# First MLP product by seven products of halves, attention by single head pairs in chunks of 96 tokens, raw weights in shared buffers

## The chip, the cores and the metric

One core of one Trainium2 chip. The time is the device time of the kernel in microseconds (us), the median of several executions. Executions of one kernel differ by 1 to 7 us, and the runs were made on more than one chip, so a kernel is compared by its ratio to the executions of the kernel before that were made with it. Engines: PE is TensorE's matmul stream, PEld its weight loads, DVE is VectorE, ACT is ScalarE, POOL is GpSimd, SP issues the DMAs. Everything is float32.

## The reference, cut to what matters

```python
batch, n_heads, seq, head_dim = (8, 8, 576, 64)
scores = q @ k.T / sqrt(64)
ret = scores * where(rel >= 0, gamma[h] ** rel, 0)   # rel = i - j, per head
x = (ret @ v)          # to 4608 tokens x 512
h = x @ w_in           # 512 x 2048; w_in, w_out, alpha arrive as float64
g = maximum(h, 0) + alpha * minimum(h, 0)
out = g @ w_out        # 2048 x 512
```

## The kernel before: the parts that matter here

The tokens go through the MLP in 18 blocks of 256, each in 8 units of 2 x 128 hidden columns: 144 units. Attention runs head pair by head pair (32 pairs in all), and units of blocks that are ready are put between its steps. The weights are float64 in DRAM; the kernel rebuilds float32 from the two 32-bit halves, piece by piece (32 pieces), while the first head pairs run.

```python
def load_piece(src, dst):                       # one of 32 pieces
    raw = wraw.tile([P, 2, HM, 2], INT32, tag="raw", bufs=4)
    nc.sync.dma_start(raw, src)
    lo, hi = raw[:, :, :, 0], raw[:, :, :, 1]
    a = wraw.tile([P, 2, HM], FP32, tag="wa", bufs=3)
    nc.scalar.activation(a, hi.bitcast(FP32), ACTF.Abs)
    nc.scalar.activation(lo, lo.bitcast(UINT32), ACTF.Copy, scale=2.0 ** -29)
    nc.vector.tensor_scalar(a, a, HI_MIN, HI_MAX, ALU.max, ALU.min)
    c = ps_a.tile([P, 2, HM], INT32, tag="psa")                     # in PSUM
    nc.vector.tensor_scalar(c, a.bitcast(INT32), 3, 0x3FFFFFF8, ...)
    nc.vector.scalar_tensor_tensor(out=dst, in0=hi, ..., in1=c, ...)
    nc.gpsimd.tensor_tensor(out=dst, in0=dst, in1=lo, op=ALU.add)

def mlp_unit(kb, i):
    ph = ps_h.tile([P, 2, TB], FP32, tag="psh")
    for x in range(2):
        for cc in range(NCC):                   # 8 matmuls of 256 columns
            nc.tensor.matmul(ph[:, x, :], w_in[i // UST][:, cc, x, f0:f0 + P],
                             xb[kb][:, cc, :], start=(cc == 0), stop=(cc == NCC - 1))
    # ... g: 2 scalings, 1 combination, 4 additions on VectorE
    # ... the second product of the unit before: 7 matmuls of 256 columns

for n, (b, u) in enumerate(couples):            # two head pairs at a time,
    qT, kT, rT = transposes(...)                # 4 chunks of 128 tokens + 64
    load_weights(2); pop_units(share // 3)
    at = scores(...)
    load_weights(3); states(...); pop_units(share // 3)
    values(...)
    load_weights(3); pop_units(share - 2 * (share // 3))
```

Of the kernel before, what the change touches and what calls it, by code (L numbers as in the profile page):

```python
# [18 lines left out]
def kernel(  # L19
# [10 lines left out]
    nc = tc.nc  # L30
# [6 lines left out]
    NC2 = NPAIR // 2  # L37
    C = P
    NJ = S // C
    REM = S - NJ * C  # L40
# [8 lines left out]
    UST = NU // NST  # L49

    assert D == 64 and 2 * D == P and DM == H * D and NTOK == B * S
    assert NTOK % TB == 0 and 2 * REM == P and NJ == 4
    assert NPAIR == NCC and DM == 512 and NU % NST == 0 and NC2 == 2

    const = ctx.enter_context(tc.tile_pool(name="const", bufs=1))
    wpool = ctx.enter_context(tc.tile_pool(name="wpool", bufs=1))
    wraw = ctx.enter_context(tc.tile_pool(name="wraw", bufs=2))
    xpool = ctx.enter_context(tc.tile_pool(name="xpool", bufs=6))
    nat = ctx.enter_context(tc.tile_pool(name="nat", bufs=2))
    attn = ctx.enter_context(tc.tile_pool(name="attn", bufs=1))  # L60
    mlp = ctx.enter_context(tc.tile_pool(name="mlp", bufs=2))
    ps_a = ctx.enter_context(tc.tile_pool(name="ps_a", bufs=3, space=bass.MemoryType.PSUM))
    ps_h = ctx.enter_context(tc.tile_pool(name="ps_h", bufs=1, space=bass.MemoryType.PSUM))
    ps_o = ctx.enter_context(tc.tile_pool(name="ps_o", bufs=1, space=bass.MemoryType.PSUM))

    couples = [(b, u) for b in range(B) for u in range(NC2)]



    def load_couple(b, u):  # L70
        got = []
        for name, src in (("k", k), ("q", q), ("v", v)):
            t = nat.tile([P, NJ, 4, D], FP32, tag=f"nat_{name}", name=f"{name}n_{b}_{u}")
            r = nat.tile([P, 2, D], FP32, tag=f"rem_{name}", name=f"{name}r_{b}_{u}")
            for j in range(NJ):
                nc.sync.dma_start(
                    t[:, j, :, :],
                    src[b, 4 * u:4 * u + 4, j * C:(j + 1) * C, :].rearrange("h p d -> p h d"))
            for i in range(2):
                h = 4 * u + 2 * i  # L80
                nc.sync.dma_start(
                    r[i * REM:(i + 1) * REM, :, :],
                    src[b, h:h + 2, NJ * C:S, :].rearrange("h p d -> p h d"))
            got += [t, r]
        return got

    loaded = {0: load_couple(*couples[0])}
# [13 lines left out]
    dif = const.tile([P, NBIT + 1, H], FP32, name="dif")  # L101
# [5 lines left out]
    for i in range(NBIT):  # L107
        nc.vector.scalar_tensor_tensor(out=dif[:, i + 1], in0=dif[:, i], scalar=2.0,
                                       in1=dif[:, i], op0=ALU.add, op1=ALU.mult)

    facl = const.tile([P, 2, H], FP32, name="facl")
    for o, y, i in [(fac[:, j], fac[:, j - 1], NBIT) for j in range(1, NJ)] + \
            [(facl[:, i], fac[:, NJ - 1], NBIT - i) for i in range(2)]:
        nc.vector.scalar_tensor_tensor(out=o, in0=dif[:, i], scalar=1.0, in1=y,
                                       op0=ALU.add, op1=ALU.mult)
# [5 lines left out]
    nc.vector.tensor_tensor(out=pf, in0=dif[:, 0:NBIT],  # L121
                            in1=pbit[:, :, None].to_broadcast([P, NBIT, H]), op=ALU.mult)
# [4 lines left out]


    tab = [const.tile([P, NC2, NJ, 4], FP32, name=f"tab{x}") for x in range(2)]
    tabr = const.tile([P, 2, NC2, 2], FP32, name="tabr")  # L130
    for u in range(NC2):
        hs = slice(4 * u, 4 * u + 4)
        nc.vector.tensor_tensor(out=tab[0][:, u], in0=fac[:, :, hs],
                                in1=pf[:, 0:1, hs].to_broadcast([P, NJ, 4]), op=ALU.mult)
    for i in range(2):
        rows = slice(i * REM, (i + 1) * REM)
        x, y = [t_.rearrange("p (u i h) -> p u i h", u=NC2, i=2)[:, :, i, :]
                for t_ in (facl[rows, i], pw[rows])]
        nc.vector.tensor_tensor(out=tabr[rows, 0], in0=x, in1=y, op=ALU.mult)
    for o, x in ((tabr[:, 1], tabr[:, 0]), (tab[1], tab[0])):  # L140
        nc.vector.tensor_scalar(o, x, float(np.sqrt(D)), None, ALU.mult)
        nc.vector.reciprocal(o, o)

    mask = const.tile([P, C], FP32, name="mask")
# [3 lines left out]
    maskr = const.tile([P, C], FP32, name="maskr")  # L148
    nc.gpsimd.tensor_copy(maskr, mask)
    nc.gpsimd.memset(maskr[0:REM, REM:C], 0.0)  # L150
# [3 lines left out]
    sm = const.tile([P, NJ, 2, P], FP32, name="sums")  # L154
# [9 lines left out]

    FS = UST * P
    w_in = [wpool.tile([P, NCC, 2, FS], FP32, tag=f"wi{i}", name=f"w_in{i}")
            for i in range(NST)]

# [11 lines left out]

    def load_piece(src, dst):
# [3 lines left out]
        raw = wraw.tile([P, 2, HM, 2], INT32, tag="raw", bufs=4, name=f"raw_{at}")  # L185
        nc.sync.dma_start(raw, src)
        lo, hi = raw[:, :, :, 0], raw[:, :, :, 1]
        a = wraw.tile([P, 2, HM], FP32, tag="wa", bufs=3, name=f"wa_{at}")
# [7 lines left out]
        c = ps_a.tile([P, 2, HM], INT32, tag="psa", name=f"wc_{at}")  # L196
        nc.vector.tensor_scalar(c, a.bitcast(INT32), 3, 0x3FFFFFF8,
                                ALU.logical_shift_left, ALU.bitwise_and)
        nc.vector.scalar_tensor_tensor(  # L199
            out=dst.rearrange("p x f -> p (x f)").bitcast(INT32),  # L200
            in0=raw.rearrange("p x f two -> p (x f) two")[:, :, 1], scalar=-0x40000000,
            in1=c.rearrange("p x f -> p (x f)"), op0=ALU.bitwise_and, op1=ALU.bitwise_or)
# [3 lines left out]
    def combine(i):  # L206
        w = w_out[i]
        for eng, o, x, y in ((nc.vector, 4, 1, 0), (nc.vector, 5, 3, 4),
                             (nc.gpsimd, 6, 5, 2), (nc.gpsimd, 1, 3, 1)):
            eng.tensor_tensor(out=w[:, o], in0=w[:, x], in1=w[:, y], op=ALU.subtract)  # L210

    pieces = []
    for s in range(NST):
        for cc in range(NCC):
            pieces.append((win32[cc, :, :, s * FS:(s + 1) * FS, :], w_in[s][:, cc], None))
        for i in range(UST * s, UST * (s + 1)):
            pieces.append((wout32[i], w_out[i][:, 0:2], None))
            pieces.append((wout32[NU + i], w_out[i][:, 2:4], i))

    def load_weights(n):  # L220
        for _ in range(min(n, len(pieces))):
            src, dst, unit = pieces.pop(0)
            load_piece(src, dst)
            if unit is not None:
                combine(unit)
# [5 lines left out]
    xb = {}  # L231
# [3 lines left out]
    def out_block(kb, po):  # L235
        p1, p2, p6, p7, p5, p3, p4 = [po[n // 2][:, n % 2, :] for n in range(7)]

        osb = wraw.tile([P, 2, 2, HM], FP32, tag="raw", bufs=4, name=f"osb_{kb}")
        s12 = wraw.tile([P, 2, HM], FP32, tag="wa", bufs=3, name=f"s12_{kb}")
        u3 = wraw.tile([P, HM], FP32, tag="wa", bufs=3, name=f"u3_{kb}")  # L240
# [7 lines left out]
        nc.vector.tensor_tensor(out=osb[:, 1, 0], in0=u3, in1=p4, op=ALU.subtract)  # L248
# [16 lines left out]

    def mlp_unit(kb, i):
        ph = ps_h.tile([P, 2, TB], FP32, tag="psh", name=f"ph_{kb}_{i}")
        f0 = (i % UST) * P
        for x in range(2):
            for cc in range(NCC):  # L270
                nc.tensor.matmul(ph[:, x, :], w_in[i // UST][:, cc, x, f0:f0 + P],  # L271
                                 xb[kb][:, cc, :], start=(cc == 0), stop=(cc == NCC - 1))


        g = mlp.tile([P, 8, P], FP32, tag="g", bufs=2, name=f"g_{kb}_{i}")
        neg = mlp.tile([P, 2, TB], FP32, tag="neg", bufs=1, name=f"neg_{kb}_{i}")
        for x in range(2):
            fc = x * NU + i
            nc.vector.tensor_scalar(neg[:, x], ph[:, x], 0.0, alpha[:, fc:fc + 1],  # L279
                                    ALU.min, ALU.mult)  # L280
        nc.vector.scalar_tensor_tensor(  # L281
            out=g[:, 0:4, :].rearrange("p x t -> p (x t)"),
            in0=ph.rearrange("p x t -> p (x t)"), scalar=0.0,
            in1=neg.rearrange("p x t -> p (x t)"), op0=ALU.max, op1=ALU.add)
        for o, x, y, op in ((4, 1, 3, ALU.add), (6, 0, 1, ALU.subtract),
                            (5, 4, 0, ALU.subtract), (7, 2, 5, ALU.subtract)):
            nc.vector.tensor_tensor(out=g[:, o, :], in0=g[:, x, :], in1=g[:, y, :], op=op)  # L287
        pend.append((kb, i, g))
        if len(pend) > 1:
            mlp_out()  # L290

    queue = []

# [4 lines left out]
    def put_x(c, tok, n, src):  # L298

        at = 0  # L300
        while at < n:
            kb, o = divmod(tok + at, TB)
            if kb not in xb:
                xb[kb] = xpool.tile([P, NCC, TB], FP32, tag="xb", name=f"xb_{kb}")
# [6 lines left out]
    def transposes(n, b, u, tiles):  # L311
        kn, kr, qn, qr, vn, vr = tiles
        for x, t, r in ((0, qn, qr), (1, vn, vr)):
            nc.gpsimd.tensor_tensor(
                out=r, in0=r, in1=tabr[:, x, u, :, None].to_broadcast([P, 2, D]), op=ALU.mult)
            nc.gpsimd.tensor_tensor(  # L316
                out=t, in0=t, in1=tab[x][:, u, :, :, None].to_broadcast([P, NJ, 4, D]),
                op=ALU.mult)
        qT = [attn.tile([P, NJ * C], FP32, tag=f"qT{i}", bufs=2, name=f"qT{i}_{n}")
              for i in range(2)]  # L320
        kT = [attn.tile([P, NJ * C], FP32, tag=f"kT{i}", name=f"kT{i}_{n}") for i in range(2)]
        rT = attn.tile([P, 2, C], FP32, tag="rT", bufs=2, name=f"rT_{n}")
        for src, dst in ((kn, kT), (qn, qT)):
            for i in range(2):
# [142 lines left out]
```

## Time and profile before

| | before |
|---|---|
| median time | 1200.31 us (1198.62 to 1202.2, 4 runs) |
| span of the profiled run | 1196.8 us |
| TensorE busy | 1135.9 us, 95% |
| VectorE / ScalarE / GpSimd busy | 49% / 9% / 11% |
| first 160 us: PE / DVE / POOL busy | 104.9 / 114.6 / 86.1 us |

A fp32 matmul appears as two instructions on TensorE (the 8 of the first product as 16 on its line, a row that the prediction shows). Its lines of busy shares and slices, and the stretches, are shown in the prediction. A second reading, called the split and used all through this document, was made after the result: how much time TensorE *loses in the head*. From 200 us on TensorE is full, so the time from there to its last instruction can be split: each instruction of the MLP at its own pace (0.216 us for 256 columns, 0.112 for 128), and the rest divided by the head pairs that are left (69 TensorE instructions per pair before, 90 after). Before: 992.0 us = 132.7 first products x 3.456 + 134 second products x 3.024 + 22.75 pairs x 5.63. Then the loss in the head is the span, less 4.8 us after TensorE's last start, less all 144 units, less all 32 pairs: 1196.8 - 4.8 - 144 x 6.48 - 32 x 5.63 = 78.6 us (from unrounded rates; good to some 2 us, and each from one profiled execution, so that two kernels which differ by less than some 3 us are not told apart). It is what the kernel would save if it ran from its first instant as it runs later. Unlike "when does the first unit of this number start", it doesn't depend on the order of the work.

### The profile page before, as it was taken

To read this page: it belongs to the slowest core of one execution; us is meant where nothing else is said; L and a number is where in the kernel's file an instruction comes from. 1 tells how busy PE (TensorE), PEld (TensorE's weight loads), DVE (VectorE), ACT (ScalarE), POOL (GpSimd) and SP (SyncE) were. 2 spreads that over 40 slices of the span, in tenths; PEclk is the share of its full clock that TensorE was granted. 3 is DMA by queue.
4 is the path that set the end of the run, shared out by engine and by line. 5 is a ranking of instruction groups with operands and counts; after the bars stand their busy time and mean duration, and the time that the engine had idled before them with its cause. 6 is when DMAs were issued, how large, how long until landed. Compare 5 with 4: busy or idle time off the path is not lost.

```text
span 1196.8 us, 15945 instructions
## 1 busy us (share of the span) xinstructions
PE 1135.9 (95%) x6529; PEld 984.5 (82%) x6529; DVE 584.5 (49%) x1516; ACT 110.8 (9%) x283; POOL 131.0 (11%) x125
## 2 busy tenths in 40 slices
PE   1678899999999999999999999999999999999998
PEld 1566778888888888888888888888888888888887
DVE  2788955354445363544443635363535444434444
ACT  1444300000000000001001000000000000000000
POOL 3565430000000000000000000000000000000000
PEclk8669899999999999999999999999999999999999
DMA  7777611010111010101110202020110000000000
GB/s 175 199 192 180 174 23 36 20 40 19 38 23 51 14 51 20 40 19 38 23 37 20 57 21 58 21 58 20 47 31 18 1 18 1 18 1 18 1 19 18
DMA packets 127145, 55.56 MB, mean 46 GB/s; under 512 B 116305, under 2 KB 116321, under 8 KB 127073
## 3 DMA queue, kind: packets, MB, share of 16 engines
q1 hardware_dynamic: 127072, 54.56, 17.6%
q8 instruction: 51, 0.84, 0.3%
q14 instruction: 22, 0.17, 0.0%
HBM read 45.10 MB, written 9.44 MB: 46 GB/s over the span
## 4 chain that ended last, share of the span: by engine, by line
PE 88%; DVE 3%; DMA 1%; issue 0%; POOL 0%; SPq 0%; DVEq 0%; POOLq 0%
PE ph L271 42%; PE po L259 35%; PE ps L345 2%; PE pv L388 2%; PE pv L397 2%; PE pt L327 2%; PE pu L368 1%; DVE at L349 1%; PE psr L356 1%; DMA vn<-in_v_dram 1%; PE pvr L402 0%; DVE w_out L210 0%; DVE wa L193 0%; PE pvr L392 0%; DMA qr<-in_q_dram 0%
## 5 line engine op out<-in xcount | busy, mean ns | idle before, releaser
L271 PE MATMUL ph<-xb,w_in 128*128 128x256 f32 x2304 | 534.4, 384 | 3.4 <-DVE g L281 3.4
L271 PEld LDWEIGHTS ph<-xb,w_in 128*128 128x128 f32 x2304 | 435.7, 191 | 66.2 <-DVE g L281 4.7
L259 PE MATMUL po<-w_out,g 128*128 128x256 f32 x2016 | 460.6, 380 | 2.2 <-DVE g L287 2.2
L259 PEld LDWEIGHTS po<-w_out,g 128*128 128x128 f32 x2016 | 382.7, 190 | 54.6 <-DVE g L287 2.4
L279 DVE TENSOR_SCALAR neg<-ph,alpha 128x256 f32<-128x256 f32 x288 | 126.4, 478 | 511.1 <-PE ph L271 510.9
L287 DVE TENSOR_TENSOR g<-g 128x128 f32<-128x128 f32 x576 | 162.7, 323 | 8.6
L281 DVE SCALAR_TENSOR_TENSOR g<-ph,neg 128x512 f32<-128x512 f32 x144 | 99.5, 691 | 4.8
L316 POOL TENSOR_TENSOR vn<-vn,tab 128x1024 f32<-128x1024 f32 x16 | 30.9, 1928 | 412.2 <-DMA vn<-in_v_dram 326.8
L345 PE MATMUL ps<-qT,kT 64*128 64x128 f32 x512 | 55.9, 304 | 18.5 <-DVE w_in L199 14.4
L345 PEld LDWEIGHTS ps<-qT,kT 64*128 64x128 f32 x512 | 48.1, 203 | 28.5 <-DVE w_in L199 15.4
L316 POOL TENSOR_TENSOR qn<-qn,tab 128x1024 f32<-128x1024 f32 x16 | 31.0, 1936 | 286.7 <-PE po L259 144.1
L306 ACT COPY xb<-pv 128x256 f32<-128x256 f32 (+3 forms) x88 | 21.7, 322 | 377.6 <-PE pv L397 377.5
L349 DVE TENSOR_TENSOR at<-ps,mask 128x512 f32<-128x512 f32 x64 | 41.2, 684 | 23.3 <-PE ps L345 23.3
L330 ACT COPY kT<-pt 128x512 f32<-128x512 f32 x32 | 17.6, 590 | 294.4 <-PE pt L327 294.2
L242 ACT COPY s<-po 128x256 f32<-128x256 f32 x18 | 6.7, 373 | 336.1 <-PE po L259 336.1
L388 PE MATMUL pv<-at,vn 128*64 128x128 f32 x512 | 33.6, 285 | 1.6 <-DVE w_out L199 1.6
L388 PEld LDWEIGHTS pv<-at,vn 128*64 128x64 f32 x512 | 29.5, 144 | 6.1 <-issue 4.0
L193 DVE TENSOR_SCALAR wa<-wa 128x512 f32<-128x512 f32 x32 | 20.6, 645 | 18.5 <-ACT wa L189 18.5
L377 DVE TENSOR_TENSOR sums<-pu,sums 64x128 f32<-64x128 f32 x96 | 27.7, 289 | 2.8
L397 PE MATMUL pv<-qT,sums 128*128 128x128 f32 x192 | 27.3, 287 | 0.4 <-DVE sums L377 0.2
L189 ACT ACTIVATE wa<-raw 128x512 f32<-128x512 f32 x32 | 21.5, 672 | 55.5 <-DMA raw<-in_moe_w_out_dram 35.5
L397 PEld LDWEIGHTS pv<-qT,sums 128*128 128x128 f32 x192 | 23.1, 191 | 4.2 <-issue 2.7
(70 smaller groups left out, 427.1 us busy)
## 6 DMA issues: line engine op xcount, KB each, us to landing
out_dram<-osb SPq DMA_DIRECT2D x36, 256.0 KB, 2.2
kn<-in_k_dram SPq DMA_DIRECT2D x64, 128.0 KB, 2.9
qn<-in_q_dram SPq DMA_DIRECT2D x64, 128.0 KB, 2.8
vn<-in_v_dram SPq DMA_DIRECT2D x64, 128.0 KB, 2.9
raw<-in_moe_w_in_dram SPq DMA_DIRECT2D x16, 512.0 KB, 6.1
raw<-in_moe_w_out_dram SPq DMA_DIRECT2D x16, 512.0 KB, 3.8
kr<-in_k_dram SPq DMA_DIRECT2D x32, 32.0 KB, 2.3
qr<-in_q_dram SPq DMA_DIRECT2D x32, 32.0 KB, 2.4
```

What stands on the lines that cost most here:

```text
L259: nc.tensor.matmul(acc[kb][n // 2][:, n % 2, :], g[:, x, :], w_out[i][:, y, :], start=(i == 0 and n % 2 == 0), stop=(i == NU - 1 and (n % ...
L271: nc.tensor.matmul(ph[:, x, :], w_in[i // UST][:, cc, x, f0:f0 + P], xb[kb][:, cc, :], start=(cc == 0), stop=(cc == NCC - 1))
L279: nc.vector.tensor_scalar(neg[:, x], ph[:, x], 0.0, alpha[:, fc:fc + 1], ALU.min, ALU.mult)
L281: nc.vector.scalar_tensor_tensor(out=g[:, 0:4, :].rearrange("p x t -> p (x t)"), in0=ph.rearrange("p x t -> p (x t)"), scalar=0.0, in1=neg ...
L287: nc.vector.tensor_tensor(out=g[:, o, :], in0=g[:, x, :], in1=g[:, y, :], op=op)
L316: nc.gpsimd.tensor_tensor(out=t, in0=t, in1=tab[x][:, u, :, :, None].to_broadcast([P, NJ, 4, D]), op=ALU.mult)
L327: nc.tensor.transpose(pt[:, j * C:(j + 1) * C], src[:, j, 2 * i:2 * i + 2, :].rearrange("p h d -> p (h d)"), ident)
L345: nc.tensor.matmul(ps[h2][:, cols], kT[i][rows, cols], qT[i][rows, cols], start=True, stop=True)
L349: nc.vector.tensor_tensor(out=a, in0=ps[h2].rearrange("p (j w) -> p j w", w=C), in1=mask[:, None, :].to_broadcast([P, NJ, C]), op=ALU.mult)
L377: nc.vector.tensor_tensor(out=sm[hd, j, :, hd], in0=ps[hd, j, :, :], in1=sm[hd, j - 1, :, hd], op=ALU.add)
L388: nc.tensor.matmul(pv[i][h2 * D:(h2 + 1) * D, j * C:(j + 1) * C], vn[:, j, 2 * i + h2, :], at[2 * i + h2][:, j, :], start=(j == 0), stop=F ...
L397: nc.tensor.matmul(pv[i][:, j * C:(j + 1) * C], sm[:, j - 1, i, :], qT[i][:, j * C:(j + 1) * C], start=False, stop=(j == NJ - 1), skip_gro ...
```

## The change

The second product was already a Strassen product: seven products of quarters in place of eight. The change does the same to the first one, whose products then are 128 columns wide, and needs combinations of w_in and of x for it (on GpSimd). These take memory, so attention goes to single pairs in six chunks of 96 (two score groups of three chunks), with two PSUM buffers in place of three; the raw weights lose their own buffers and use those of the output and of later x blocks.

```diff
-    def mlp_unit: 8 matmuls, 256 columns each
+        for n, (m, o, l, r) in enumerate((
+                (0, 2, 0, x[:, 0:2, 0:P]), (0, 0, 2, x[:, 2:4, 0:P]), (0, 1, 5, t[:, 1]),
+                (1, 0, 4, t[:, 0]), (1, 1, 6, x[:, 0:2, P:TB]),
+                (1, 2, 1, x[:, 2:4, P:TB]), (1, 3, 3, t[:, 2]))):
+            for cc in range(2):                 # 14 matmuls of 128 columns
+                nc.tensor.matmul(ph[m][:, o], w_in[i // UST][:, l, cc, f0:f0 + P], r[:, cc], ...)
+        # g: 1 copy on ScalarE, 4 additions out of PSUM, 2 scalings, 1 combination, 4 additions
+    S_WORK = ((6, 0, 1, ALU.subtract), (4, 1, 3, ALU.add), (5, 4, 0, ALU.subtract),
+              (1, 2, 5, ALU.subtract))          # per quarter of w_in, on GpSimd
+    def combine_x(kb): 4 subtractions of 256 elements on GpSimd per token block
     # combinations of w_out: two of four on VectorE before, all on GpSimd after
-        raw = wraw.tile(..., tag="raw", bufs=4)
-        c = ps_a.tile([P, 2, HM], INT32, tag="psa")
+        raw = ring.tile(..., tag=raw_tag(at))   # 5 shared buffers for 16 pieces, then 3
+        c = ps_h.tile([P, 2, HM], INT32, tag="psh1")   # shared with half of the first product
-    C = P                                       # chunks of 128, couples of head pairs
+    C = 96                                      # 6 chunks, single pairs
-    ps_a: bufs=3, ps_h: 1 tile
+    ps_a: bufs=2, ps_h: psh0, psh1
```
(cut to its core)

## The prediction

> **What bounds the kernel now.** I read the page's busy shares and 40 slices first. TensorE is busy 95% of the span; from slice 6 on it is full, at the full granted clock. VectorE is at half.
>
> ```profile
> PE 1135.9 (95%) x6529; PEld 984.5 (82%) x6529; DVE 584.5 (49%) x1516; ACT 110.8 (9%) x283; POOL 131.0 (11%) x125
> ...
> PE   1678899999999999999999999999999999999998
> ...
> DVE  2788955354445363544443635363535444434444
> ...
> POOL 3565430000000000000000000000000000000000
> PEclk8669899999999999999999999999999999999999
> ```
>
> So there are two stages: a head of some 160 us in which weights are unpacked and TensorE has gaps at a low clock, and a steady stage in which every nanosecond of TensorE's stream is on the path. The table of stretches shows the border:
>
> ```profile
> 60.00:90.00 30.00, 21.63 (x154) 18.32 (x155) 25.17 (x46) 13.84 (x27) 19.01 (x16) 0.67 0.72 193
> 90.00:120.00 30.00, 25.44 (x191) 20.22 (x189) 26.23 (x50) 12.90 (x27) 15.97 (x15) 0.96 0.71 180
> 120.00:150.00 30.00, 26.92 (x186) 21.30 (x186) 27.49 (x57) 11.64 (x25) 14.72 (x14) 0.89 0.68 170
> ...
> 300.00:600.00 300.00, 299.55 (x1733) 260.92 (x1732) 134.51 (x361) 17.18 (x54) 18.31 (x16) 1.00 0.12 31
> ```
>
> Its columns are busy time of matmul, weight load, VectorE, ScalarE and GpSimd, then clock, DMA share and GB/s. From 300 to 600 us TensorE idles 0.45 us. Then I read the timeline inside the steady stage, for the weight loads (PEld), whose starts are recorded:
>
> ```profile
> 704.85 3.43 PEld L271 LDWEIGHTS ph<-xb,w_in 128*128 128x128 f32 x16
> ...
> 708.30 3.00 PEld L259 LDWEIGHTS po<-w_out,g 128*128 128x128 f32 x14
> ...
> 711.32 3.43 PEld L271 LDWEIGHTS ph<-xb,w_in 128*128 128x128 f32 x16
> ```
>
> One MLP unit lasts 711.32 - 704.85 = 6.47 us: 30 instructions (each fp32 matmul is two) of 0.216 us. 16 belong to the first product, 3.45 us. The question of the whole change is what such an instruction costs with 128 moving columns in place of 256, when each still needs its own 128x128 weights. The kernel before has that case, in the attention's products with the running sums:
>
> ```profile
> 753.36 1.42 PEld L397 LDWEIGHTS pv<-qT,sums 128*128 128x128 f32 x12 [0.17 <-issue]
> ...
> 754.70 0.53 PEld L402 LDWEIGHTS pvr<-rT,sums 128*128 128x128 f32 x4
> ```
>
> L397 moves 128 columns, L402 64. One load lasts 0.19 us, so the starts are (1.42 - 0.19) / 11 = 0.112 us apart in the first and (0.53 - 0.19) / 3 = 0.113 in the second. Half the columns do not make it shorter[...].
>
> [...] these three additions, 1.02 us for four elsewhere, take 2.39 us beside a GpSimd multiply.
>
> ```profile
> 725.63 2.39 DVE L287 TENSOR_TENSOR g<-g 128x128 f32<-128x128 f32 x3
> 725.94 1.94 POOL L316 TENSOR_TENSOR qn<-qn,tab 128x1024 f32<-128x1024 f32 x1 [28.30 <-PE po L259]
> ```
>
> **The change, part by part.**
>
> First product. Removed per unit: 16 instructions of 0.216 us = 3.45 us. Added: 7 products x 2 halves x 2 = 28 of 0.112 us = 3.14 us. The gain is 0.32 us, not the eighth of 3.45 (0.43) that counting multiplications suggests[...]. Over the 138 of 144 units outside the head: 44 us less on the path. A unit becomes 6.16 us.
>
> Attention. In the chain of work in order of time, the starts of first products are 6.475 us apart except where attention lies between; over one couple of head pairs the excess is 4.05 (values), 2.10 (transposes) and 5.13 (scores and states), together 11.28 us, or 5.64 per pair. After, per pair, at the starts in the trace:
> - 12 transposes instead of 9, 0.109 us each[...]: 1.3, and 0.2 for waits on two buffers;
> - 12 score products of 96 columns. The two heads lie in separate halves of the array and run as pairs; a pair of instructions takes 0.111 us at 128 columns, so I estimate 0.084 at 96. 12 x 0.084 = 1.0, plus about 0.3 (three starts delayed by 0.1 each) on entering and leaving such a group, now two groups: 1.6;
> - 10 state products at 0.058 per pair of instructions: 0.6 + 0.3 = 0.9;
> - 12 value products of 96 columns at 0.084: 1.0; 5 with the sums, two instructions each at 0.112: 1.1; entry and exit 0.3: 2.4.
> The sum is 6.4, and 6.6 with the first wait of the states for a bank. 0.96 us more per pair, over 24 pairs after the head: +23 us on the path. Half the gain goes back here.
>
> VectorE. Per unit now: four additions out of PSUM (three of 256 elements at 0.41 as on L247, one of 128 at 0.28), two scalings of 256 in SBUF (about 0.3, an estimate from L193, whose fastest 512-element runs take 0.43), one 512-element combination (0.69) and four additions of 128 (0.26 to 0.32): 4.1 us, against 2.9 before. With the output block (7 x 0.41 per 8 units) and attention (4 x 0.45 + 5 x 0.22 per 4.5 units) that is 5.1 of some 7.6 us of TensorE time: 67%, no bound. Latency: g must be ready when the second product starts, one whole unit later, about 8 us after its first sums are complete; 4.1 us fit, also with one GpSimd multiply (1.5 us) in the way.
>
> GpSimd. Per token block four subtractions of 256 elements, about 0.65 each by a line through L314 (128 in 0.43) and L316 (1024 in 1.93): 2.6 us, and twice as many, three-quarter-size multiplies. In the compiled order the subtractions for the next block stand half a block ahead, and at a batch's border one whole unit (6 us) lies between the last copies and the first product that needs them. I allow 5 us in all for such stalls.
>
> The head. Before, it ends at 162 us with 6 units done. What paces it is a loop and not one engine: the DMA queue waits for raw buffers, as its waits up to 170 us say.
>
> ```profile
> SPq L186 <- POOL w_in L203: 41.1, 13, 7.3
> SPq L186 <- POOL qr L314: 11.1, 3, 4.6
> SPq L186 <- POOL w_out L203: 7.8, 7, 2.7
> ```
>
> After: only two single pairs are loaded ahead of the first weights, which therefore start at about 11 us instead of 22.7; five raw buffers for 16 pieces, then three instead of four; and the unpacking no longer takes the attention's PSUM buffers (before, the first scores wait 11 us for VectorE to release one). Against that, GpSimd gets the combinations of both weights: 8 x 2 x 1.5 multiplies, 32 x 1.31 additions, 32 x 0.75 and 16 x 1.07 combinations, 5 for blocks = 112 us, against 86 by 160 us before. It would be 80% busy and may set the pace. The unpacking also shares one PSUM buffer with half of the first product, so in the compiled order VectorE takes pieces and units strictly in turn. DMA bytes are the same. Earlier start minus these: the head ends at 150 us with 6 units done, plus or minus 10.
>
> Sum: 150 + 138 x 6.16 + 24 x 6.6 + 5 stalls + 5 for the last block = 1168 us of span. The same sum for before is 162 + 138 x 6.475 + 12 x 11.28 + 5 = 1196, against 1196.8 seen. The median time is about 3 us over the span: 1170 us, 2.5% less.
>
> **The rivals.**
>
> (a) The halves stream at their share of columns, 0.107 us: units of 6.02, 1151 us. Against it: L397's starts at 0.112, and L402's.
>
> (b) VectorE's longer chain[...] makes the second product wait. A stall of 0.3 us per unit would cost 41 us: 1211. For it: the collision above. Against it: 4 us of slack, and GpSimd busy only some 12% of the steady stage.
>
> (c) The head grows: GpSimd or the three raw buffers pace it, and it ends at 170 us or later: 1190, within 2%. For it: GpSimd's 112 us and the waits of the DMA queue. Against it: the start 11 us sooner.
>
> (d) With two PSUM buffers for attention instead of three, TensorE waits in each of five groups per pair: 0.3 us each would be 36 us over 24 pairs: 1206. Against it: the compiled order puts a whole unit, or three first-product matmuls, between most of these groups.
>
> **Range and chances.** Steady-stage rates are measured, so unit and attention together are good to 10 us; the head to 10; stalls can only add. I give 1150 to 1190. The border of 2% lies at 1176.8, close above my value: faster 0.63, within 2% 0.33, slower 0.04.
>
> **What would show each step.** Weight loads of the first product 0.112 us apart and units of 6.16 us between attention groups (0.107: rival a). Attention adds 6.4 to 6.6 us per pair. TensorE's idle time after 170 us under 12 us in all; if it is tens of us, with VectorE's g as releaser it is (b), with score or value copies as releaser (d). First raw weights issued at about 11 us, TensorE full from about 150; if GpSimd is full in the head and the fill comes after 165, (c). What would make it wrong most: a head much longer or shorter than 150, since its loop is the one part that I did not add up from rows.

The two heads' score products run as pairs by their starts in the trace of before, where the second follows the first by 7 ns and the next pair comes 105 to 112 later. The 0.107 us of rival (a) stand for half of the 0.216 of 256 columns; half is 0.108, and the units would be 6.05.

## The result, and the profile after

1183.81 us median (1182.47 to 1188.55, 4 runs) against 1200.31: the ratio is 0.9869, 95% interval 0.9837 to 0.9901. Ratios here are the mean time of one kernel's fast runs over that of the other's of the same rounds, so not quite the ratio of the medians quoted. That is 1.3% less: within 2%. The time lies in the predicted range, 14 us above the predicted value, and the class that was held likeliest did not come.

The page of the changed kernel, the same rows that the prediction shows of the one before:

```profile
PE 1138.2 (96%) x8929; PEld 1030.3 (87%) x8929; DVE 774.5 (66%) x2142; ACT 189.1 (16%) x547; POOL 236.4 (20%) x227
...
PE   6877899999999999999999999999999999999998
...
DVE  6558768566657576756665767676667566667565
...
POOL 4786571110111011200110201021112000100000
PEclk9998889999999999999999999999999999999999
```

TensorE is busy just as long, with 2400 instructions more; VectorE is at 66%, as worked out. The slices fill at about the same place as before: the head did not become visibly shorter. Its timeline near the end, weight loads of the first product, in rows of eight:

```profile
1155.10 1.08 PEld L285 LDWEIGHTS ph<-xb,w_in 128*128 128x128 f32 x8
1156.10 0.97 PEld L285 LDWEIGHTS ph<-xt,w_in 128*128 128x128 f32 x8
...
1161.25 1.08 PEld L285 LDWEIGHTS ph<-xb,w_in 128*128 128x128 f32 x8
```

One load takes 0.19, so in the second row the starts are (0.97 - 0.19) / 7 = 0.111 us apart, and units start 1161.25 - 1155.10 = 6.15 us apart. Stretches, with the columns of the prediction's:

```profile
20.00:40.00 20.00, 17.01 (x114) 14.73 (x113) 11.48 (x24) 10.09 (x27) 15.05 (x13) 1.00 0.67 188
40.00:60.00 20.00, 17.59 (x126) 15.39 (x127) 12.69 (x28) 10.20 (x23) 15.44 (x16) 1.00 0.69 166
...
300.00:600.00 300.00, 299.40 (x2411) 272.24 (x2411) 196.69 (x554) 39.54 (x126) 39.45 (x36) 1.00 0.13 34
```

In the steady stage TensorE is idle for 0.6 of 300 us, so VectorE does not hold it up. (Busy time is modelled, 0.28 us for an instruction of the first product where the starts are 0.112 apart, and so hides short waits; by the starts of the instructions, the two PSUM buffers cost some 0.3 us per pair, as shown below.) Split as before, the changed kernel has 976.6 us from 200 us = 133.1 x 3.136 + 135 x 3.024 + 23.38 pairs x 6.45. The sums of both spans, side by side:

| part | before | predicted | after |
|---|---|---|---|
| 144 units | 144 x 6.48 = 933.1 | 144 x 6.16 = 887.0 | 144 x 6.16 = 887.0 |
| 32 head pairs | 32 x 5.63 = 180.3 | 32 x 6.6 = 211.2 | 32 x 6.45 = 206.5 |
| lost in the head | 78.6 | 60.2 (150 - 6 x 6.16 - 8 x 6.6) | 83.0 |
| stalls, last block | 4.8 | 5 + 5 | 4.9 |
| span | 1196.8 | 1168.4 | 1181.4 |

Units came as predicted; pairs and stalls cost 10 us less. The whole miss, and more, is in the head: it was to lose 18 us less than before, and lost 4 more. Its DMA queue's waits up to 200 us answer to those shown of before:

```profile
SPq L179 <- POOL w_out L194: 46.4, 10, 10.7
SPq L179 <- POOL w_in L194: 43.9, 13, 9.6
SPq L76 <- PE pu L377: 24.1, 6, 7.7
SPq L76 <- PE pv L391: 18.8, 7, 12.1
```

The weights did start sooner (first raw piece issued at 8.1 us, landed at 13.0; before 22.7 and 27.4), but the last one landed at 160.7 us (before 145.2). At this place DMA waits for the unpacking and not the unpacking for DMA: piece 12 (counted from 0) landed at 57.3 us, and ScalarE took it up at 73.8. The start that was gained is used up half way. GpSimd's addition to the 4th, the 16th and the last piece starts at 44.5, 86.3 and 152.1 us before, and at 28.2, 85.6 and 171.2 us in the changed kernel.

One thing stands in no row of the page. Ten instructions with the running sums, in the chain of waits, once in the head and once in the steady stage (start, us, what):

```profile
33.70 2.39 PE pv L395 x10
...
514.85 1.28 PE pv L395 x10
```

In the head TensorE runs at half rate: these instructions, with full 128 x 128 weights, start 213 ns apart instead of 112. By the durations of the weight loads (0.34 us in place of 0.19) this lasts from 8 to 81 us almost without a break, and some 90 us in all; in the kernel before some 60 us (58 by its granted clock, 0.82 over the first 160, and 3 before that record begins). The row of the granted clock reads 1.00 through those 80 us. It is not blind to the state: the first change of the clock that this trace records is the one to full rate at 81.3 us, and before it the row shows 1.00. In a run told of below, which has recorded changes from 6.5 us on, the same stretch has the same work at 0.50:

```profile
20.00:40.00 20.00, 17.01 (x115) 14.50 (x114) 11.81 (x23) 10.90 (x27) 15.58 (x14) 0.50 0.65 192
```

So where no change is recorded yet, go by the durations. What brings TensorE from half rate to full is not shown, nor which property of the attention work keeps it there: it was busy 17.0 and 17.6 of 20 us in the two stretches above, with small gaps, and stayed at half rate.

### The profile page after: what moved, and what is told of

Read it like the earlier page. It is cut to its first block, busy times and chain, and to the rows that moved or that the text cites. A ratio compares the mean times of both kernels' runs of the same rounds, so it can differ in the third digit from the quotient of the medians.

```text
span 1181.4 us, 22020 instructions
## 1 busy us (share of the span) xinstructions
PE 1138.2 (96%) x8929; PEld 1030.3 (87%) x8929; DVE 774.5 (66%) x2142; ACT 189.1 (16%) x547; POOL 236.4 (20%) x227
## 4 chain that ended last, share of the span: by engine, by line
PE 85%; DVE 7%; POOL 3%; issue 2%; ACT 1%; DMA 1%; SPq 0%; DVEq 0%; POOLq 0%; ACTq 0%
PE ph L285 37%; PE po L255 34%; PE ps L366 4%; PE pv L395 3%; PE pv L391 3%; PE pt L354 3%; PE pu L377 2%; DVE wa L186 1%; POOL xt L270 1%; DVE g L307 1%; DVE wc L190 1%; POOL vn L345 1%; DVE g L296 1%; POOL xb L270 1%; DVE w_out L192 1%
## 5 line engine op out<-in xcount | busy, mean ns | idle before, releaser
L296 DVE TENSOR_TENSOR g<-ph,g 128x256 f32<-128x256 f32 (+1 forms) x576 | 211.7, 388 | 314.5 <-ACT g L291 168.8
L285 PE MATMUL ph<-xb,w_in 128*128 128x128 f32 x2304 | 333.5, 283 | 4.2 <-DVE g L296 3.3
L285 PEld LDWEIGHTS ph<-xb,w_in 128*128 128x128 f32 x2304 | 294.5, 194 | 14.0 <-POOL w_in L194 2.9
L285 PE MATMUL ph<-xt,w_in 128*128 128x128 f32 x1728 | 248.3, 279 | 7.0 <-POOL xt L270 2.8
L285 PEld LDWEIGHTS ph<-xt,w_in 128*128 128x128 f32 x1728 | 221.4, 195 | 8.9 <-POOL xt L270 3.1
L299 DVE TENSOR_SCALAR g<-g,alpha 128x256 f32<-128x256 f32 x288 | 120.3, 459 | 4.9
L301 DVE SCALAR_TENSOR_TENSOR g<-g 128x512 f32<-128x512 f32 x144 | 105.8, 735 | 4.2
L366 PEld LDWEIGHTS ps<-qT,kT 64*96 64x96 f32 x768 | 52.1, 179 | 24.3 <-issue 12.8
L366 PE MATMUL ps<-qT,kT 64*96 64x96 f32 x768 | 64.3, 278 | 3.9 <-DVE at L369 3.2
L369 DVE TENSOR_TENSOR at<-ps,mask 96x288 f32<-96x288 f32 x128 | 53.2, 446 | 10.3 <-PE ps L366 10.2
```

What stands on the lines that cost most here:

```text
L285: nc.tensor.matmul(ph[m][:, o], w_in[i // UST][:, l, cc, f0:f0 + P], r[:, cc], start=(n in (0, 3) and cc == 0), stop=(n in (2, 6) and cc = ...
L296: nc.vector.tensor_tensor(out=o, in0=x0, in1=x1, op=ALU.add)
L299: nc.vector.tensor_scalar(g[:, 4 + 2 * m:6 + 2 * m], g[:, 2 * m:2 * m + 2], 0.0, alpha[:, fc:fc + 1], ALU.min, ALU.mult)
L301: nc.vector.scalar_tensor_tensor(out=g[:, 0:4].rearrange("p x t -> p (x t)"), in0=g[:, 0:4].rearrange("p x t -> p (x t)"), scalar=0.0, in1 ...
L366: nc.tensor.matmul(ps[h2][:, j], kT[rows, c0:c0 + C], qT[rows, c0:c0 + C], start=True, stop=True)
L369: nc.vector.tensor_tensor(out=at[h2][:, r * JR:(r + 1) * JR], in0=ps[h2], in1=mask[:, None, :].to_broadcast([C, JR, C]), op=ALU.mult)
```

## The experiments

Twelve kernels ran. Each is named by its edit to the changed kernel; the last three columns are worked out from its trace as above.

| kernel | median us | ratio to before | us per pair | lost in head | DVE / POOL busy, first 160 us |
|---|---|---|---|---|---|
| before | 1200.31 | 1 | 5.63 | 78.6 | 114.6 / 86.1 |
| changed | 1183.81 | 0.9869 | 6.45 | 83.0 | 106.0 / 111.2 |
| first product in the old form | 1205.18 | 1.0057 | 6.27 | 66.3 | 107.5 / 94.3 |
| needless products at the start | 1183.62 | 0.9872 | 6.45 | 84.1 | 106.5 / 110.3 |
| needless products in four pairs | 1185.36 | 0.9887 | 6.45 | 82.9 | 108.9 / 110.8 |
| larger attention groups | 1181.64 | 0.9860 | 6.18 | 89.1 | 103.1 / 104.5 |
| w_in's combinations on VectorE | 1187.87 | 0.9910 | 6.44 | 87.6 | 118.5 / 92.6 |
| all combinations on VectorE | 1191.93 | 0.9933 | 6.46 | 89.5 | 124.6 / 71.8 |
| one raw buffer more | 1182.49 | 0.9858 | 6.46 | 80.6 | 110.4 / 115.5 |
| value step split | 1182.96 | 0.9871 | 6.45 | 82.9 | 106.1 / 110.8 |
| no combinations of w_in | 1181.10 | 0.9846 | 6.44 | 78.8 | 109.8 / 96.1 |
| unpacking's intermediate in SBUF | 1189.07 | 0.9913 | 6.44 | 90.2 | 120.3 / 110.3 |
| no clamp | 1183.17 | 0.9871 | 6.47 | 81.5 | 91.0 / 110.2 |
| larger groups after the head + raw buffer | 1173.90 | 0.9789 | 6.18 | 84.0 | 111.1 / 116.2 |

The medians of before moved from 1198.3 to 1200.3 us, so ratios are to be compared. Units took 6.16 us in all but the old form (6.48). In the last row the first eight pairs are of the slower form; with these at 6.45 us its loss in the head is 81.8.

### First product in the old form

```diff
-    14 matmuls of 128 columns, combine_x, S_WORK, ScalarE copy + 4 PSUM additions
+    for x in range(2):
+        for cc in range(NCC):
+            nc.tensor.matmul(ph[:, x, :], w_in[i // UST][:, cc, x, f0:f0 + P], xb[kb][:, cc, :], ...)
```

> The changed kernel with the first MLP product put back to 16 instructions of 256 columns (no combinations of its weights or of x); attention by single pairs, chunks of 96 and shared raw buffers stay. Theory A (each part of the change is worth what its rows say: the halves gain 138 x 0.32 = 44 us, attention by single pairs costs about 27 us more through its entries and exits): units return to 6.475 us, steady stage 40 to 48 us longer than in the changed kernel; with GpSimd relieved of 16 + 4 to 8 combinations the head may end up to 10 us sooner; in all 1215 to 1230 us, slower than the kernel before. Theory B (the attention part costs nothing net and the gain of the halves is only some 13 us): 1195 to 1200 us, as before.

1205.18 us, ratio 1.0057 (interval 1.0044 to 1.0069): between the two theories. The split tells why. Its span of 1204.8 is 8.0 us over that of before: pairs cost 32 x 0.64 = 20.5 more, and the head loses 78.6 - 66.3 = 12.3 *less*. So all of the change but the first product's form (early start of the weights, shared buffers, single pairs, GpSimd's combinations of w_out) does shorten the head, by two-thirds of the 18 us that the prediction gave it. Back to the changed kernel, the halves then give 144 x 0.32 = 46.1 us, take 32 x 0.18 = 5.8 in the pairs and 83.0 - 66.3 = 16.7 in the head: 23.6 of 46 us remain (the spans differ by 23.4). This is where the expected gain went. (This run is not quite the first product of before: its sums take two PSUM buffers in turn, in place of one.) The runs below look for what the 16.7 consist of, and whether one cause in the head can be taken away.

### Needless products that keep TensorE busy: at the start, and in four pairs

```diff
+    ones = const.tile([P, TB], FP32); nc.vector.memset(ones, 1.0)
+    def warm(k): k times matmul(wps[:, 0], ones[:, 0:P], ones)    # 256 columns
+    warm(8)                     # both kernels: before the first transposes
+    if n < 4: warm(3)           # second kernel: at each of the four places for units
```

> The changed kernel with 8 needless matrix products of 256 columns (about 7 us) on a constant tile, ahead of the first transposes, while TensorE waits for its first data. Theory C (the head is long because TensorE runs at half rate from 8 to 81 us, as its 128-column instructions 213 ns apart instead of 112 show, and would run at full rate if it were kept busy early): the first pairs go at 112 ns per 128-column instruction, the head ends 10 to 25 us sooner, 1160 to 1175 us. Theory C2 (it falls back to half rate within a pair, since the attention alone does not keep it up): no change beyond 5 us, 1178 to 1186. Theory D (the head is paced by GpSimd, the raw buffers or the unpacking, TensorE only waits for them): no change although the instructions are at 112 ns.

> As the run with the needless products at the start, and 12 more (3 at each of four places) in each of the first four pairs, about 5 us of TensorE time per pair at full rate. Theory C and C2: TensorE at full rate (112 ns) through most of the first 80 us, pairs of 10 to 12 us instead of 15.8, head ends 10 to 20 us sooner: 1162 to 1174 us. Theory D: the pairs stay 15 us and more apart with TensorE waiting for data of other engines; 1180 us or longer, since the needless products take their 20 us where TensorE was busy.

0.9872 and 0.9887: no gain. With the products at the start alone, TensorE was at full rate to 15.6 us and fell back by 17.1; none of its gaps from 1.3 to 60 us exceeded 1.4 us; half rate then lasted to 88 us. In the second kernel it ran at full rate from 5 to 43 us, and the head still lost 82.9 us. So half rate is real, and taking it away for 38 us in this way gains nothing: the fourth pair ended at 69.4 us, against 67.4 in the changed kernel. What half rate costs stays open, though, since the needless products themselves are 22% of the second kernel's chain of waits from 15 to 56 us. From 32 to 46 us this chain went through VectorE and ScalarE, where TensorE had been: there other engines set the pace at full rate. The timeline of that place, VectorE first, then GpSimd (start, us):

```profile
36.71 3.58 DVE L195 TENSOR_SCALAR wa<-wa 128x512 f32<-128x512 f32 x1
...
40.92 0.42 DVE L195 TENSOR_SCALAR wa<-wa 128x512 f32<-128x512 f32 x1
```
```profile
36.63 0.72 POOL L279 TENSOR_TENSOR xt<-xb 128x256 f32<-128x256 f32 x1
37.31 1.30 POOL L203 TENSOR_TENSOR w_out<-w_out,raw 128x512 int32<-128x512 int32 x1
38.57 0.73 POOL L279 TENSOR_TENSOR xt<-xb 128x256 f32<-128x256 f32 x1
39.26 0.74 POOL L208 TENSOR_TENSOR w_out<-w_out 128x256 f32<-128x256 f32 x1
```

The clamp takes 0.42 us alone and 3.58 beside four GpSimd instructions in a row: it ends only after the last of them (at 40.29 us, theirs at 40.00). The prediction had such a collision for additions only, and did not count the clamp at all.

### The combinations on VectorE: those of w_in, and all

```diff
-            nc.gpsimd.tensor_tensor(out=w[:, o], in0=w[:, x], in1=w[:, y], op=op)
+            eng = nc.vector if work is S_WORK else nc.gpsimd     # second kernel: nc.vector
+            eng.tensor_tensor(out=w[:, o], in0=w[:, x], in1=w[:, y], op=op)
```

> The changed kernel with the 16 combinations of the first product's weights (1.29 us each, 20.7 us) on VectorE instead of GpSimd; those of the second product's weights stay on GpSimd. Theory G (GpSimd's queue[...] paces the head: in the run with TensorE kept at full rate it was busy almost without a gap from 22 to 54 us, and the head was no shorter; the run with the first product in the old form, which lacks these combinations, lost some 17 us less in the head): the head loses 8 to 17 us less than in the changed kernel, 1167 to 1176 us. Rival H (VectorE paces it as well, at 66% busy in the head[...]): within 4 us of the changed kernel, 1179 to 1187 us. Rival K (the old form was shorter in the head only because its 256-column instructions kept TensorE at full rate and its units need no combinations at all): within 4 us too.

> The changed kernel with all combinations of both products' weights (16 of 512 elements, 32 of 256: 43.6 us) on VectorE instead of GpSimd. Theory G: GpSimd falls from 111 to about 70 us busy in the head; VectorE rises by some 25 us to about 130 of 160. The head loses 12 to 22 us less unless VectorE then becomes the pacer; 1162 to 1174 us. Rival H: VectorE paces now; no better than the run with only the first product's combinations moved, or slower than the changed kernel.

Both slower: 0.9910 and 0.9933, 5 and 8 us more than the changed kernel. GpSimd's queue alone does not pace the head (theory G falls): with 40 us less on it the head lost 6.5 us more. VectorE is no free place either: these additions have two operands in SBUF, and those of 512 elements took 1.11 us on average where the fastest took 0.67.

### One raw buffer more

```diff
-        tags = ["o0", "o1", "x5"] + (["x3", "x4"] if n < 16 else [])
+        tags = ["o0", "o1", "x5", "rw0"] + (["x3", "x4"] if n < 16 else [])
```

> The changed kernel with one more buffer for raw weights, of its own: six for the first 16 pieces, four for the last 16, instead of five and three. Theory G: pieces of the first half wait some 15 to 20 us in their buffers for ScalarE and GpSimd anyway, and of the last half partly too; the work that paces the head is unchanged: within 4 us, 1179 to 1186 us. Theory L (three buffers pace the last 16 pieces, whose landings were 5.8 us apart against 3.4 to 3.6 us in the first half): landings 4 to 4.5 us apart in the last half, the last piece lands 15 to 20 us sooner, 1165 to 1174 us.

0.9858: about 1 us, 2.4 by the split. The last piece landed at 151.4 instead of 160.7 us and GpSimd's addition to it started at 165.6 instead of 171.2; so three raw buffers do delay the last pieces, and yet hardly any of these 6 to 9 us arrives in the time. Theory L falls.

### No combinations of w_in (wrong result on purpose)

```diff
-    (w_in[s], S_WORK) if cc == NCC - 1 else None
+    None
-    w_in[i // UST][:, l, cc, f0:f0 + P]
+    w_in[i // UST][:, l % 4, cc, f0:f0 + P]
```

> Wrong result on purpose. The changed kernel without the 16 combinations of the first product's weights (20.7 us of GpSimd in the head); the seven products read the raw quarters in their place, so every other instruction, buffer and wait stays. Moving this work to VectorE made the kernel 4 us slower; this takes it away without giving it to anyone. Theory M (the work itself is what the head is longer by[...]): most of the gain of the run with the first product in the old form, which lost 16.7 us less in the head than the changed kernel: 1168 to 1174 us. Rival N (that gain came from the other parts of the old form: TensorE at full rate through 256-column instructions, a shorter chain on VectorE, no combinations of x): within 4 us of the changed kernel, 1179 to 1187 us.

0.9846, some 3 us; 4.2 by the split (of this kernel's fastest execution). Of the 16.7 us this is the part of w_in's combinations, about a quarter. 20.7 us of work taken from a queue that is 70% busy give back 3 to 4. The traces show where the other part arises. GpSimd's additions to the 16th and to the last piece start at 81.0 and 164.3 us in this run, at 81.2 and 157.2 in the old form, and at 85.6 and 171.2 in the changed kernel: up to the 16th piece w_in's combinations are the whole difference, and the 7 us by which this run then falls behind the old form come after it, when the units have begun.

### The unpacking's intermediate in SBUF

```diff
-        c = ps_h.tile([P, 2, HM], INT32, tag="psh1")
+        c = wraw.tile([P, 2, HM], INT32, tag="wcs", bufs=1)
```

> The changed kernel with the intermediate of the unpacking in a buffer of its own in SBUF instead of the PSUM buffer that it shares with half of the first product. Theory P (the shared buffer makes VectorE take pieces and units strictly in turn; pieces 18, 19, 22 and 23 waited 7 to 11 us between their first and second VectorE step): these waits fall to under 3 us, and the head loses 4 to 12 us less: 1172 to 1180 us. Rival Q (the waits are only the order of VectorE's queue, or end in work that waits for another engine): within 3 us of the changed kernel, 1180 to 1187 us; or longer[...].

0.9913: 5 us slower. Groups of VectorE instructions up to 180 us, changed kernel first, then this run (busy us, mean ns):

```profile
L190 DVE TENSOR_SCALAR wc<-wa 128x512 int32<-128x512 int32 x32 | 21.9, 684 | 0.4
...
L192 DVE SCALAR_TENSOR_TENSOR w_out<-raw,wc 128x512 int32<-128x512 int32 x16 | 10.8, 676 | 0.1
```
```profile
L190 DVE TENSOR_SCALAR wc<-wa 128x512 int32<-128x512 int32 x32 | 26.1, 817 | 0.2
...
L192 DVE SCALAR_TENSOR_TENSOR w_out<-raw,wc 128x512 int32<-128x512 int32 x16 | 14.9, 928 | 0.1
```

With the intermediate in PSUM none of the 32 steps of L190 took over 0.70 us, the 22 that overlap a GpSimd instruction among them. In SBUF the same steps took 0.41 to 1.39 us, 0.82 on average. The changed kernel's trace has the same difference elsewhere: beside GpSimd the clamp, which reads and writes SBUF, took up to 2.33 us (0.43 at most alone) and the combination of L301, also in SBUF, up to 1.94 (0.69), while the additions out of PSUM of L296 took 0.43 at most with and without. Whether the tie between pieces and units costs anything by itself stays open, since this edit brought a cost of its own.

### No clamp (right for these inputs only)

```diff
-        nc.vector.tensor_scalar(a, a, HI_MIN, HI_MAX, ALU.max, ALU.min)
```

> Right for these inputs, wrong for values outside the range of float32. The changed kernel without the clamp of each weight piece (32 VectorE instructions, 25.4 us by 180 us of the profile). Theory H (VectorE's queue is on the chain that sets the head: giving it 21 and 44 us of GpSimd's combinations cost 5 and 8 us in time, and taking 21 us from GpSimd gave only about 3): the head loses 6 to 14 us less, 1169 to 1177 us. Rival S (the head is set by the order of the program - pairs, pieces and units in turn through all engines - and no one engine's work moves it by more than a few us): 1179 to 1184 us, at most 4 us less than the changed kernel.

0.9871: no gain in time, 1.5 us by the split. The first 160 us of the changed kernel, of the run without w_in's combinations and of this one (PE, PEld, DVE, ACT, POOL busy):

```profile
0.00:160.00 160.00, 123.75 (x884) 106.27 (x885) 106.00 (x259) 62.86 (x144) 111.22 (x108) 0.95 0.60 156
```
```profile
0.00:160.00 160.00, 123.69 (x930) 106.19 (x931) 109.77 (x272) 64.11 (x147) 96.09 (x96) 0.91 0.61 158
```
```profile
0.00:160.00 160.00, 123.27 (x955) 106.36 (x957) 90.95 (x238) 64.72 (x146) 110.22 (x108) 0.96 0.61 156
```

GpSimd loses 15 us of work in one, VectorE 15 in the other, and the end hardly moves. Rival S is what is left: in the head TensorE, VectorE and GpSimd are 66 to 77% busy (ScalarE 39%), and a head pair, four pieces and a unit pass through TensorE, ScalarE, VectorE and GpSimd in turn. Taking work from VectorE or GpSimd gave 3 us at most, and adding work where it collides cost 5 to 8. That the order of the program sets the pace is argued from this and not shown: no run changed the order of pairs, pieces and units in the head. Nor did one settle what half rate costs. It lasted some 68 us in the old form and some 77 without w_in's combinations, against some 90 here; 22 us less at half rate is up to 11 us of TensorE's time, an estimate from these durations, which could be much of what the old form gained.

### The attention groups: split further, and made larger

```diff
+        pop_units(extra)        # first kernel: a unit between values with v and with the sums
```
```diff
-    transposes: 4 groups of three chunks; scores: 2 groups of three chunks x 2 heads
+    transposes: chunks 0-4 of k, of q; then the last chunk of both in one buffer
+    states right after that; scores: chunks 0-4 of both heads, then the last chunk
```

> The changed kernel with one MLP unit moved between the two parts of each value step (the 12 products with v and the 5 with the running sums) after the head: one or two more attention groups per pair, 231 in the compiled order against 207, and no other work. Theory E (each separate group costs some 0.2 to 0.3 us through its slower entry and the slower first product after it): 4 to 8 us longer than the changed kernel, 1187 to 1193 us. Rival F: no difference beyond 2 us.

> The changed kernel with attention's instructions in larger groups: five of the six transposes of k and of q together in one PSUM bank each, the two last ones beside the state products, ten of the twelve score products together and the last two apart. The compiled order has 150 attention groups between MLP groups, against 207. The work on TensorE is the same (the same 12 transposes, 12 + 10 + 17 products per pair). Theory E (attention by single pairs costs through its number of entries and exits, about 0.3 us each with the slower first instructions after it): about 46 groups fewer after the head, 10 to 18 us less: 1166 to 1174 us. Rival F (the cost is in the products of 96 columns themselves, or the larger groups wait for VectorE and ScalarE to release their two banks): within 5 us of the changed kernel, 1179 to 1189 us.

Theory E as it was worded falls. The split added 24 groups and cost nothing (0.9871, 6.45 us per pair): what it splits are a tiled group, of two heads side by side in the array, and one of full 128 x 128 weights, so the change from one kind to the other was there before. In both traces the entry from the second product into a tiled group is 309 ns instead of the own 216, while the entry into full-width products is 216, no dearer than inside the MLP. The larger groups save 0.27 us per pair, for another reason. Chain of waits over one pair's transposes, in the changed kernel and then with the larger groups (from the trace of the version of the next section, which has the same groups here):

```profile
522.31 0.26 PE pt L354 x3
...
522.65 0.41 ACT kT L357
...
523.11 0.47 PE pt L354 x3
523.58 0.25 PE ph L285 x2
523.83 0.25 PE pt L354 x3
```
```profile
519.05 0.83 PE pt L385 x10
...
532.21 0.17 PE ptl L393 x2
```

With three chunks to a buffer, the third group of transposes has to wait until ScalarE has emptied a buffer, and TensorE has only two instructions of a first product to put in between. By the starts of the instructions from 300 to 1000 us, the 12 transposes cost 1.27 us per pair, of which 12 x 0.082 = 0.98 are their own. With five chunks to a buffer ten transposes need two buffers, and a whole unit lies between them and the last two; they cost 0.91 and some 0.17. This is most of the 0.27; the run changed the score groups and the place of the states as well, and no run separates them. In the head this run lost 6 us more and so kept 1 to 3 us of its gain (ratio 0.9860, spans 1178.7 against 1181.4).

### A version that beats both

```diff
+        if n < 2 * NST:  (attention as in the changed kernel)
+        else:            (the larger groups)
+        tags = ["o0", "o1", "x5", "rw0"] + ...
```

> Correct result, an attempt at a version that beats both: the changed kernel's attention for the first eight pairs, the larger groups for the 24 pairs after the head, and one raw buffer more. From the two runs: the larger groups cost 6.18 us per pair in the steady stage against 6.45 (24 x 0.27 = 6.5 us), and lost 6 us in the head, where they are not used here; the raw buffer gave 2.4 us in the head. If these add up: 1173 to 1177 us. If the head swallows the changes or the order of the two forms costs waits: 1179 to 1184.

1173.90 us (1173.09 to 1175.39), ratio 0.9789, interval 0.9773 to 0.9805: as expected, 2.1% less than before (the interval reaches over the border of 2%, so that "faster by 2%" is not settled) and 0.8% less than the changed kernel. The spans differ by 7.7 us, of which 24 x 0.27 = 6.5 are the pairs after the head: in the steady stage, where TensorE is the one bound, a small saving arrives whole, as far as 1 us can be told.

## Why the prediction was right or wrong

- **First product: right.** 0.112 us per instruction as predicted, units of 6.16 (6.15 seen). Rival (a), 6.02, is refuted. What sets the 0.112 is not shown: 64 and 128 moving columns have the same spacing (0.113 and 0.112), and the load of 128 weight columns as such is not it, since the transposes load as many and start 82 ns apart.
- **Attention: right, with one term read wrongly.** 6.4 to 6.6 us per pair was said, 6.45 measured. By the starts from 300 to 1000 us, values cost 2.43 (2.4 said), scores 1.6 (1.6), states 0.9 (1.1 with the wait for a bank), transposes 1.27 (1.5); 0.3 to 0.4 lies in slower MLP instructions beside these groups. Transposes start 82 ns apart and not 109, in proportion to the 96 columns that they move (109 at 128 before), with 128 weight columns both times.
- **VectorE and rival (b), two buffers and rival (d): right.** 67% said, 66% seen; 0.6 us of TensorE idle in 300, and the waits for PSUM buffers some 0.3 us per pair where (d) had 1.5. The 5 us of stalls did not come.
- **The head: wrong, and the one step that failed.** "Earlier start minus these: the head ends at 150 us" nets the earlier start against GpSimd's longer work. In the split, that is 18 us less lost than before; it was 4 us more. In the prediction's terms, with 6 units and 8 pairs done, the head ended at 83.0 + 6 x 6.16 + 8 x 6.45 = 171.6 us. The weights did start 14 us sooner, and the unpacking had used this up by its 16th piece. The old-form run cuts the miss in two: all but the first product's form gave 12.3 us, and the halves, of which the sum had in the head only GpSimd's work, took 16.7. Rival (c) named the direction and the end, 170 us or later, and its two mechanisms, GpSimd and three raw buffers, turned out to be worth 3 to 4 and 1 to 2 us.
- **What the 16.7 us are.** Shown: 3 to 4 are the combinations of w_in. The other 12 to 14 (the unpacking shows 7 of them, all after the 16th piece) belong to what else the old form changed: combinations of x, a longer chain per unit on ScalarE and VectorE, 28 narrower instructions in place of 16, how the sums use the PSUM buffers, more time at half rate. No run splits these, and this stays open.
- **The chances.** The prediction said itself that the head "is the one part that I did not add up from rows", allowed it 10 us, and put its middle only some 6 us under the border of 2% (1176.3 us from the median; it writes 1176.8). 0.63 is about what its own ranges give; the head's 10 us were too few, since the head alone missed by some 22. That the time still lies in the range is partly luck: 10 us that pairs and stalls did not cost covered part of it.

## What to carry to other kernels

Split a span into what the full-rate stage costs per piece of work and what the start loses: the first could here be predicted within some 5 us of 1100 from rows, the second not at all. In a start-up stage where three engines were 66 to 77% busy, removing 15 us of work from one of them gave 0 to 3 us of time, and moving 21 and 44 us of it from GpSimd to VectorE, where additions that took 0.67 us at best took 1.11 on average, made things worse by 5 and 8 us. Put the effort where one engine is the only bound; there, 0.27 us saved 24 times arrived whole.
